# Moving two more GELU tiles to PSUM, and one more group of softmax heads to VectorE, in a fused attention and MLP kernel

## The chip, the cores and the metric

The kernel runs on one core of one Trainium2 chip. The core has TensorE (matmuls, PE in the profile), ScalarE (activation functions, ACT), VectorE (DVE), GpSimd (POOL) and SyncE (SP, which issues most DMAs). The metric is the device time of one execution in microseconds; the figure for the kernel before is the median of seven runs.

## The reference

The input x has 2048 rows of 448. After a layer norm (no learned scale), two branches are computed and combined:

```python
xn = _layernorm(x, axis=-1)
s = _A_ref(xn, A_wqkv, A_wo)                       # attention, 16 heads of 28
g = _silu(_B_ref(xn, B_w1, B_b1, B_w2, B_b2))      # MLP 448 -> 1792 -> 448
return x + s * g

# inside _A_ref
scores = jnp.einsum("bhqd,bhkd->bhqk", q, k) * scale
p = _softmax(scores, axis=-1)
o = jnp.einsum("bhqk,bhkd->bhqd", p, v)
# inside _B_ref
h = _gelu(jnp.einsum("bsd,df->bsf", x, w1) + b1)
return jnp.einsum("bsf,fd->bsd", h, w2) + b2
```

The scores are 16 x 2048 x 2048 numbers, each of which needs one exp.

## The kernel before, in words

**Tiling.** The scores are cut into 1024 pieces of 128 keys x 512 queries, called heads here and `m` in the code. A block is one group of four attention heads (`g`) and one chunk of 512 queries (`c`); there are 16 blocks of 64 heads, numbered in the order of work. Within a block four consecutive `m` are the same key tile for four attention heads, so that four numbers `4*q ... 4*q+3` form a group.

**Two ways to an exp.** Most heads go to ScalarE. `p_scores` lets TensorE write two or three heads side by side into one half of a PSUM ring of six banks (line 1217), and `p_exps` reads them with one exp and writes them as bf16 into a P slot (line 1273). The halves are banks 0 to 2 and 4 to 5, used in turn, so that the exps hold three and two heads in turn (only two while the first 64 heads are done). The groups named in `QUADS` go to VectorE in place of ScalarE. For each, `p_late` has single scores written to any free PSUM bank, or has them join a waiting task of `p_scores`; `p_apass` reads each bank once (line 1376), and `p_expq` makes an exp out of bit operations and a polynomial in five passes over 128 x 2048 numbers (lines 1427 to 1434). A group needs three work areas (`unit`), which are parts of buffers whose first use is over: x, w2 before it is loaded, the q and k weights, kT of blocks that are done. `step` leaves those groups out of the order of `p_scores`.

**PV and the end.** `p_pv` multiplies P by V into one PSUM bank (`acc`), eight heads at a time (line 1488). Groups from VectorE are added when they are ready, at the latest at the end of their block. Then the block is normalised, and after the last block of four the output projection is done (line 1585).

**The MLP.** The first layer makes 56 tiles of 128 x 512 (4 chunks x 14). The table of functions for gelu is another than the one for exp, so that all gelus run at once, in one stage in the middle, at about head 582 (`GM`). Before that stage, 36 of the tiles have been computed while exps ran, and VectorE has copied them from PSUM to `h` in SBUF (`p_f1`, line 1069). The other 20 are computed during the stage by `p_direct` (line 1086) into the ring, which no scores use then, and gelu reads them straight from PSUM. `PIECES` gives the order of gelu: an SBUF piece of five or four tiles, then a PSUM group (`None`) of three or two, and so on (`p_gelu`, line 1131). A PSUM group can be filled when the group two before it, which had the same half of the ring, has been read. Line 1136 loads the table for exp again. Then `p_f2` does the second layer beside the exps of the later blocks (line 1152), and `p_silu` makes the gate with a tanh (line 1167).

**Memory that is shared.** The part of `h` whose tiles come straight from PSUM isn't used before the gelu stage; until head 558 it gives 20 extra P slots beside the 18 of `P` (`pslots`, `p_room`). `room_free` holds the first PSUM gelu back until these have been used by PV. After gelu, xnT gives 15 more P slots.

**Order of work.** The program has no loops on the chip. A planner in Python (`run`, `start_of`, `put`) takes, of all tasks that could come next, the one with the earliest estimated start, and among those within 0.1 us the one with the lowest rank. Ranks that matter here: gelu -1, single scores for VectorE 0.9, scores for ScalarE 1, exp 3, direct tiles 3.5, first-layer tiles and second layer 5, PV 6 (1.2 when it lags far behind). When TensorE has been idle, filler matmuls on zeros (line 902) are put in by `p_busy`. In the gelu stage groups of VectorE may be begun up to 48 heads ahead (`GLEAD`). What the planner decides becomes a fixed order on each engine with semaphore waits between them, so a change of one list can alter the order of everything after it.

Of the kernel before, what the change touches and what calls it, by code (L numbers as in the profile page):

```python
# [19 lines left out]
C = 4  # L20
KT = 4
T = 16
FT = F // 128
WS = D + 4
NRING = 6
NP = 18
# [1 line left out]
MTOT = NBLK * T * 4  # L28

GM = 64 * 9 + 6  # L30
QUADS = (17, 22, 25, 35, 36, 50, 54, 65, 76, 84, 89, 99, 102, 116, 118, 132, 140, 142, 145, 152, 153, 162, 164, 179, 186, 194, 204, 210, 211, 214, 228, 233, 243)
SM_SCALE = DH ** -0.5
LOG2E = 1.4426950408889634
EXP_A3, EXP_A2, EXP_LC = 0.16391228, 0.00783292, 1.1187538523466403
# [2 lines left out]
KNORM = 2.5  # L37
PV_START = 5
HAM_WIN, HAM_LOW, DUM = 3.4, 0.85, 0.17
ND = 8  # L40
PIECES = [(0, 0, 5), None, (0, 5, 5), None, (0, 10, 4), None, (1, 0, 5), None, (1, 5, 5), None, (1, 10, 4), None,
          (2, 0, 4), None, (3, 10, 4), None]
SBT = [(c, ft) for c, f0, n in [p for p in PIECES if p] for ft in range(f0, f0 + n)]
SEM, OWN = 0.07, 0.03
SWITCH = 0.1
JOINT = 0.05
# [27 lines left out]
class _Kernel:  # L74
# [183 lines left out]
    def alloc(self):  # L258
# [3 lines left out]
        B = _Buf  # L262
# [99 lines left out]
        self.b_ox = [B() for _ in range(C)]  # L362
        hx = lambda c, f0, n: self.h[:, c, 512 * f0:512 * (f0 + n)].rearrange("p (k n) -> p k n", n=512)
        self.pslots = [(self.P[:, i0:i0 + n, :], k) for i0, n in ((0, NP),) for k in range(n)]
        self.pslots += [(hx(c, f, 10), k) for c, f in ((2, 4), (3, 0)) for k in range(10)]
        self.pslots += [(self.xnT[:, :, :].rearrange("p k (c n) -> p (k c) n", n=512), k) for k in range(16)]
        self.b_P += self.b_hf[2][4:14] + self.b_hf[3][0:10] + [B() for _ in range(16)]
        self.pon = [(0, NP)]
        self.b_nm = [[B(), B()] for _ in range(C)]
        self.b_selb = B()  # L370
# [13 lines left out]
    def schedule(self):  # L384
# [27 lines left out]
        K.pv_done = [False] * MTOT  # L412
        K.late = {4 * q + k for q in QUADS for k in range(4)}
        K.late_left = [sum(1 for q in QUADS if K.sub_of(4 * q) == b) for b in range(NBLK + 3)]
        K.late_on = False
# [24 lines left out]
        def nxt():  # L440
            nonlocal o
            o += 1.0
            return o
# [18 lines left out]
        K.spawn(K.p_qn(1), nxt())  # L462
        f1 = deque(SBT)
        for c in range(C):
# [625 lines left out]

    def directs(self):
        K = self
        out, left = [], [[2, 4], [3, 0]]
        for i in range(ND):
            b0 = 4 * ((K.gu - 1 + i) % 2)
            n = 2 if b0 else 3
            c, f0 = left[i // (ND // 2)]
            left[i // (ND // 2)][1] += n
            out.append((c, f0, n, b0))
        return out  # L1100

    def p_direct(self):
        K = self
        yield ("until", lambda: K.gu is not None and K.exp_u >= K.gu - 1)
        for i, (c, f0, nf, b0) in enumerate(K.directs()):
            yield ("until", lambda: K.exp_u >= K.gu - 1 + i if i < 2 else K.dir_read >= i - 1)
            for n in range(nf):
                for k in range(2):
                    yield K.t_f1(c, f0 + n, K.ring[:, b0 + n, :], K.b_ring[b0 + n], k, 3.5)
            K.dir_n += 1  # L1110

    def p_gelu(self):
        K = self
        yield ("until", lambda: K.gu is not None and K.exp_u >= K.gu and K.n_f1 == len(SBT))
        left = [FT] * C
        for q, pc in enumerate(PIECES):
            if pc:
                c, f0, n = pc
                src = K.h[:, c, 512 * f0:512 * (f0 + n)]
                rd = []  # L1120
            else:
                i = K.dir_read
                yield ("until", lambda: K.dir_n > i and K.room_free())
                c, f0, n, b0 = K.directs()[i]
                src = K.ring[:, b0:b0 + n, :].rearrange("p b n -> p (b n)")
                rd = K.b_ring[b0:b0 + n]
                for ft in range(f0, f0 + n):
                    K.hf_free(c, ft)
            dst = K.h[:, c, 512 * f0:512 * (f0 + n)]
            left[c] -= n  # L1130
            yield _Task(ACT, lambda eng, dst=dst, src=src: eng.activation(dst, src, ACTF.Gelu_apprx_tanh), rd,  # L1131
                        K.b_hf[c][f0:f0 + n] + ([K.b_h[c]] if left[c] == 0 else []),
                        0.4267 * n + (0.1 if pc else 0.06) + (1.3 if q == 0 else 0), 0.05, -1)
            if not pc:
                K.dir_read += 1
        K.prog[ACT].append(lambda eng: eng.preload_act_table_set("exp_and_others"))
        K.tE[ACT] += 1.3
        for b in K.b_fsb + K.b_sig:
            b.w = K.b_w1.w
            b.r = list(K.b_w1.r) + [K.b_w1pad.w] + K.b_w1pad.r  # L1140
        K.gelu_done = True

    def p_f2(self, c, t):
        K = self
        bank, tok = yield ("bank", lambda: K.b_h[c].tw is not None and K.ready([K.b_h[c], K.b_w2]) and K.dir_read == ND and (c < 2 or K.g_done[c - 2]))
        hv = K.h[:, c, :].rearrange("p (f n) -> p f n", n=512)
# [83 lines left out]
    def p_scores(self):  # L1230
        K = self
        u = 0
        while K.next_m < MTOT:
# [3 lines left out]
            if K.gu is not None and u == K.gu + 1:  # L1237
                yield ("until", lambda: K.dir_read == ND)
            b0 = 4 * (u % 2)
# [103 lines left out]
    def in_gelu(self):  # L1343
        return self.gu is not None and self.exp_u >= self.gu - 1 and self.dir_read < ND

    def p_late(self):
        K = self
        yield ("until", lambda: K.late_on)
        K.spawn(K.p_room(), 0)
        for q in QUADS:  # L1350
            m0 = 4 * q
# [30 lines left out]
    def p_room(self):  # L1382
        K = self
        yield ("until", lambda: K.stg_done == 2)
        for ft in range(10):
            K.hf_free(3, ft)
        K.pon += [(NP, 10), (NP + 10, 10)]
        yield ("until", lambda: K.next_m >= GM - 24)
        K.pon = K.pon[:1]
        yield ("until", lambda: K.gelu_done)  # L1390
        for b in K.b_P[NP + 20:]:
            for x in K.b_xnT:
                for y in x:
                    b.r += y.r
        K.pon.append((NP + 20, 15))

    def room_free(self):
        K = self
        return all(K.pv_done[m] for i, m in K.plast.items() if NP <= i < NP + 20)

    def assign(self, ms, b0):
        K = self
# [274 lines left out]
```

## Time and profile before

| | before |
|---|---|
| median of 7 runs | 462.34 us (462.14 to 462.75) |
| the profiled execution | 462.15 us |
| its span, first to last instruction | 460.3 us |
| busy: ScalarE, TensorE, VectorE | 448.5, 438.3, 368.1 us |
| exps (line 1273) | 363 instructions, 892 heads |
| gelus (line 1131) | 8 from SBUF, 8 from PSUM |
| gelu stage, table load to the first exp after | 245.2 to 273.1 us |
| granted TensorE clock | 0.998 of full speed |

Times in the profile are from the start of the span. A line of a group gives source line, engine, operation, tiles written and read, sizes and count; then the time in which any of the group was busy, the mean of one in ns, and the engine's idle time ahead of them with what ended it. Consecutive instructions of ScalarE overlap in the record: one ends after the next has begun. "h", "xnT" and "P" as the target of an exp are only the place of its P slot.

### The profile page before, as it was taken

How to read it: one execution, taken by the hardware profiler on the slowest of the kernel's cores; microseconds unless marked ns; L12 is line 12 of the kernel's file. 1: busy time of each engine (PE TensorE's matmuls, PEld its weight loads, DVE VectorE, ACT ScalarE, POOL GpSimd, SP SyncE). 2: the span in 40 equal slices, each digit the busy share in tenths (PEclk: the TensorE clock that was granted, in tenths of full speed). 3: DMA queues.
4: the chain of work that ended last, by engine and by line, in shares of the span. 5: the costliest groups of instructions: out<-in, count | busy, mean ns of one | idle time of the engine just before them, and what ended most of it. 6: DMA issues, size and time to landing. Idle time of an engine off the chain costs nothing.

```text
span 460.3 us, 10628 instructions
## 1 busy us (share of the span) xinstructions
PE 438.3 (95%) x4474; PEld 164.7 (36%) x4474; DVE 368.1 (80%) x577; ACT 448.5 (97%) x408; POOL 42.4 (9%) x85
## 2 busy tenths in 40 slices
PE   6999999999999999999999999999999999999995
PEld 5533333333323332323323333333333244343462
DVE  8956898898888898968888997157878689989675
ACT  6999999999999999999999999999999999999994
POOL 7470000001010000000000000000000100101011
PEclk9999999999999999999999999999999999999999
DMA  9701000000000000000040000000000010111131
GB/s 266 269 2 37 2 1 0 1 2 3 2 1 1 1 0 3 2 1 2 1 140 1 1 0 3 2 2 0 1 1 1 1 41 2 22 21 15 28 43 41
DMA packets 8048, 11.16 MB, mean 24 GB/s; under 512 B 1697, under 2 KB 6993, under 8 KB 7954
## 3 DMA queue, kind: packets, MB, share of 16 engines
q1 hardware_dynamic: 6850, 8.43, 6.0%
q0 software_dynamic: 864, 1.38, 2.3%
q8 instruction: 35, 0.57, 0.5%
q10 hardware_dynamic: 288, 0.69, 0.4%
q14 instruction: 11, 0.09, 0.1%
HBM read 8.61 MB, written 3.21 MB: 26 GB/s over the span
## 4 chain that ended last, share of the span: by engine, by line
PE 52%; ACT 34%; issue 10%; DVE 2%; DMA 1%; POOL 0%; ACTq 0%; DVEq 0%; POOLq 0%
ACT P L1273 16%; PE ring L1217 14%; ACT h L1273 11%; PE acc L1488 10%; PE ring L1086 6%; ACT xnT L1273 5%; PE ring L1152 4%; PE misc L1152 4%; PE acc L902 3%; PE misc L1086 2%; PE ring L741 1%; PE misc L741 1%; PE misc L1217 1%; PE misc L1585 1%; PE ring L1585 1%
## 5 line engine op out<-in xcount | busy, mean ns | idle before, releaser
L1273 ACT ACTIVATE P<-ring 128x1024 bf16<-128x1024 f32 (+1 forms) x194 | 224.0, 1264 | 1.1 <-PE ring L1217 0.8
L1217 PE MATMUL ring<-qT,kT 32*128 32x512 bf16 (+2 forms) x1072 | 142.5, 358 | 11.2 <-ACT P L1273 4.4
L1273 ACT ACTIVATE h<-ring 128x1024 bf16<-128x1024 f32 (+1 forms) x98 | 115.7, 1303 | 0.2
L1217 PEld LDWEIGHTS ring<-qT,kT 32*128 32x128 bf16 x1072 | 37.2, 91 | 133.3 <-ACT P L1273 57.9
L1273 ACT ACTIVATE xnT<-ring 128x1536 bf16<-128x1536 f32 (+1 forms) x71 | 84.8, 1286 | 0.1
L1488 PE MATMUL acc<-P,vaug 128*32 128x512 bf16 (+2 forms) x537 | 50.6, 357 | 0.4 <-ACT P L1273 0.4
L1086 PE MATMUL ring<-xnT,w 128*128 128x512 bf16 x152 | 40.2, 382 | 0.1
L1558 POOL CAST rhi<-rc 128x16 bf16<-128x16 f32 x15 | 6.9, 457 | 358.9 <-DVE rc L1556 194.5
L902 PE MATMUL acc<-ident,zero 128*128 128x128 bf16 x444 | 36.3, 220 | 0.0
L902 PEld LDWEIGHTS acc<-ident,zero 128*128 128x128 bf16 x444 | 25.3, 98 | 15.0 <-issue 13.6
L1217 PE MATMUL misc<-qT,kT 32*128 32x512 bf16 (+1 forms) x80 | 29.6, 374 | 0.0
L1376 DVE TENSOR_SCALAR x_sb<-misc 128x512 uint16<-128x512 f32 x34 | 23.3, 686 | 7.6 <-PE misc L1217 7.0
L1152 PE MATMUL misc<-w,h 128*128 128x448 bf16 x112 | 27.6, 356 | 0.2 <-DVE wk L1376 0.2
L1152 PE MATMUL ring<-w,h 128*128 128x448 bf16 x112 | 27.2, 355 | 0.3 <-DVE qT L980 0.3
L1488 PE MATMUL acc<-h,vaug 128*32 128x512 bf16 x243 | 25.9, 385 | 0.0
L1488 PE MATMUL acc<-xnT,vaug 128*32 128x512 bf16 (+2 forms) x236 | 21.2, 331 | 0.0
L1086 PE MATMUL misc<-xnT,w 128*128 128x512 bf16 x72 | 20.2, 383 | 0.0
L1546 DVE CAST E_sb<-acc 128x512 bf16<-128x512 f32 x15 | 10.4, 691 | 10.6 <-PE acc L1488 10.4
L1488 PEld LDWEIGHTS acc<-P,vaug 128*32 128x32 bf16 x537 | 13.0, 95 | 15.4 <-issue 11.1
L1086 PEld LDWEIGHTS ring<-xnT,w 128*128 128x128 bf16 x152 | 11.6, 97 | 17.5 <-issue 6.8
L1131 ACT ACTIVATE h<-h 128x2560 bf16<-128x2560 bf16 (+1 forms) x8 | 17.1, 2131 | 0.0
L1376 DVE TENSOR_SCALAR kT<-ring 128x512 uint16<-128x512 f32 x18 | 12.4, 686 | 5.6 <-PE ring L1217 5.6
(262 smaller groups left out, 655.0 us busy)
## 6 DMA issues: line engine op xcount, KB each, us to landing
w<-in_B_w_dram SPq DMA_DIRECT2D x1, 1568.0 KB, 7.3
w<-in_B_w_dram SPq DMA_DIRECT2D x1, 1344.0 KB, 8.8
out_dram<-in_A_x_dram SPq DMA_DIRECT2D x3, 448.0 KB, 11.9
out_dram<-h POOLq DMA_DIRECT2D x6, 224.0 KB, 3.9
x_sb<-in_A_x_dram SPq DMA_DIRECT2D x2, 448.0 KB, 5.1
h<-in_A_wqkv_dram SPq DMA_DIRECT2D x3, 168.0 KB, 4.9
x_sb<-in_A_x_dram ACTq DMA_DIRECT2D x1, 448.0 KB, 4.8
h<-in_A_x_dram SPq DMA_DIRECT2D x1, 448.0 KB, 3.4
```

Source lines behind the costliest of these rows:

```text
L741: ins = eng.matmul(bank, w[:, kt, g * 128:(g + 1) * 128], K.xnT[:, kt, c * 512:(c + 1) * 512], start=(kt == 0), stop=(kt == KT - 1))
L902: ins = eng.matmul(K.acc[:, 0:128], K.zero[:, :], K.ident[:, :], start=False, stop=True, skip_group_check=True)
L1086: ins = eng.matmul(bank, K.w1[:, kt, ft * 128:(ft + 1) * 128], K.xnT[:, kt, c * 512:(c + 1) * 512], start=(kt == 0), stop=(kt == KT - 1))
L1131: yield _Task(ACT, lambda eng, dst=dst, src=src: eng.activation(dst, src, ACTF.Gelu_apprx_tanh), rd, K.b_hf[c][f0:f0 + n] + ([K.b_h[c]] if ...
L1152: ins = eng.matmul(ps, hv[:, ft, t * 128:(t + 1) * 128], K.w2[:, ft, :], start=(ft == 0), stop=(ft == FT - 1))
L1217: return eng.matmul(dst, K.kT[32 * j:32 * j + 32, g, t * 128:(t + 1) * 128], K.qT[32 * j:32 * j + 32, g, c * 512 + q0:c * 512 + q0 + nq], ...
L1273: return eng.activation(reg[:, i0:i0 + n, :], K.ring[:, b0:b0 + n, :], ACTF.Exp, scale=SM_SCALE)
L1376: yield _Task(DVE, lambda eng: eng.tensor_scalar(K.unit[u][:, 512 * k:512 * k + 512].bitcast(dt.uint16), bank, SM_SCALE * LOG2E * 128.0, ( ...
L1488: return eng.matmul(K.acc[32 * j:32 * j + 32, q0:q0 + nq], K.vaug[:, t, 4 * g + j, :], ap[:, col:col + nq], tile_position=(0, 32 * j), sta ...
L1546: yield _Task(DVE, lambda eng: eng.tensor_copy(E, K.acc[:, :]), [K.b_acc], [tE], 0.7, 0.0, 0)
L1558: yield _Task(POOL, lambda eng: eng.tensor_copy(K.rhi[:, :], K.rc[:, :]), [K.b_rc], [K.b_rhl], 1.1, 0.0, 1)
L1585: ins = eng.matmul(ps, K.qT[:, g, c * 512 + t * 128:c * 512 + (t + 1) * 128], K.wo[:, g, :], start=(g == 0), stop=(g == G - 1))
```

## The change

- PSUM groups of gelu: nine in place of eight (`ND`), with 22 tiles in place of 20. Groups alternate between three and two tiles, and the last takes what is left.
- SBUF pieces: 34 tiles in place of 36, in pieces of 5, 5, 5, 4, 4, 4, 4, 3. Pieces now run over the flat index of the 56 tiles and may cross a chunk's border; the tiles from PSUM are the last 22. The last two gelus are both PSUM groups.
- The extra P slots before gelu are 22 (8 + 14) in place of 20 (10 + 10).
- `QUADS`: 34 groups in place of 33. Twelve are kept (17, 22, 25, 36, 65, 99, 142, 152, 153, 164, 194, 211), 22 have new places. Blocks 3, 8 and 9 have one, four and four groups in place of two, three and three; the other blocks have as many as before.

```diff
-QUADS = (17, 22, 25, 35, 36, 50, 54, 65, 76, 84, 89, 99, 102, 116, 118, 132, 140, 142, 145, 152, 153, 162, 164, 179, 186, 194, 204, 210, 211, 214, 228, 233, 243)
+QUADS = (17, 22, 25, 36, 37, 59, 65, 72, 82, 87, 99, 103, 115, 122, 129, 135, 138, 142, 152, 153, 157, 158, 164, 168, 178, 180, 194, 199, 211, 213, 222, 229, 234, 242)
...
-ND = 8
-PIECES = [(0, 0, 5), None, (0, 5, 5), None, (0, 10, 4), None, (1, 0, 5), None, (1, 5, 5), None, (1, 10, 4), None,
-          (2, 0, 4), None, (3, 10, 4), None]
-SBT = [(c, ft) for c, f0, n in [p for p in PIECES if p] for ft in range(f0, f0 + n)]
+ND = 9
+PIECES, F0 = [], 0
+for n in (5, 5, 5, 4, 4, 4, 4, 3):
+    PIECES += [(F0, n), None]
+    F0 += n
+PIECES += [None] * (ND - PIECES.count(None))
+SBT = [(f // FT, f % FT) for f in range(F0)]
...
-        self.pslots += [(hx(c, f, 10), k) for c, f in ((2, 4), (3, 0)) for k in range(10)]
+        self.pslots += [(hx(2, F0 - 28, 42 - F0), k) for k in range(42 - F0)] + [(hx(3, 0, 14), k) for k in range(14)]
...
     def directs(self):
         K = self
-        out, left = [], [[2, 4], [3, 0]]
+        out, f = [], F0
         for i in range(ND):
             b0 = 4 * ((K.gu - 1 + i) % 2)
-            n = 2 if b0 else 3
-            c, f0 = left[i // (ND // 2)]
-            left[i // (ND // 2)][1] += n
-            out.append((c, f0, n, b0))
+            n = min(2 if b0 else 3, 56 - f)
+            out.append((f, n, b0))
+            f += n
+        assert f == 56
         return out
...
-        K.pon += [(NP, 10), (NP + 10, 10)]
+        K.pon += [(NP, 42 - F0), (NP + 42 - F0, 14)]
...
-        return all(K.pv_done[m] for i, m in K.plast.items() if NP <= i < NP + 20)
+        return all(K.pv_done[m] for i, m in K.plast.items() if NP <= i < NP + 56 - F0)
```

`p_direct` and `p_gelu` are changed to the flat index in the same way.

More of the change, by code (lines that the diff above doesn't have):

```diff
@@ L364, in alloc @@
         self.pslots = [(self.P[:, i0:i0 + n, :], k) for i0, n in ((0, NP),) for k in range(n)]
-        self.pslots += [(hx(c, f, 10), k) for c, f in ((2, 4), (3, 0)) for k in range(10)]
+        self.pslots += [(hx(2, F0 - 28, 42 - F0), k) for k in range(42 - F0)] + [(hx(3, 0, 14), k) for k in range(14)]
         self.pslots += [(self.xnT[:, :, :].rearrange("p k (c n) -> p (k c) n", n=512), k) for k in range(16)]
-        self.b_P += self.b_hf[2][4:14] + self.b_hf[3][0:10] + [B() for _ in range(16)]
+        self.b_P += self.b_hf[2][F0 - 28:14] + self.b_hf[3] + [B() for _ in range(16)]
         self.pon = [(0, NP)]
@@ L1104, in p_direct @@
         yield ("until", lambda: K.gu is not None and K.exp_u >= K.gu - 1)
-        for i, (c, f0, nf, b0) in enumerate(K.directs()):
+        for i, (f0, nf, b0) in enumerate(K.directs()):
             yield ("until", lambda: K.exp_u >= K.gu - 1 + i if i < 2 else K.dir_read >= i - 1)
@@ L1108, in p_direct @@
                 for k in range(2):
-                    yield K.t_f1(c, f0 + n, K.ring[:, b0 + n, :], K.b_ring[b0 + n], k, 3.5)
+                    yield K.t_f1((f0 + n) // FT, (f0 + n) % FT, K.ring[:, b0 + n, :], K.b_ring[b0 + n], k, 3.5)
             K.dir_n += 1
@@ L1115, in p_gelu @@
         left = [FT] * C
+        hf = K.h[:, :, :].rearrange("p c f -> p (c f)")
         for q, pc in enumerate(PIECES):
             if pc:
-                c, f0, n = pc
-                src = K.h[:, c, 512 * f0:512 * (f0 + n)]
+                f0, n = pc
+                src = hf[:, 512 * f0:512 * (f0 + n)]
                 rd = []
@@ L1123, in p_gelu @@
                 yield ("until", lambda: K.dir_n > i and K.room_free())
-                c, f0, n, b0 = K.directs()[i]
+                f0, n, b0 = K.directs()[i]
                 src = K.ring[:, b0:b0 + n, :].rearrange("p b n -> p (b n)")
                 rd = K.b_ring[b0:b0 + n]
[L1127 to L1130, printed above, removed]
+                for f in range(f0, f0 + n):
+                    K.hf_free(f // FT, f % FT)
+            dst = hf[:, 512 * f0:512 * (f0 + n)]
+            for f in range(f0, f0 + n):
+                left[f // FT] -= 1
+            wr = [K.b_hf[f // FT][f % FT] for f in range(f0, f0 + n)]
+            wr += [K.b_h[c] for c in range(C) if left[c] == 0 and K.b_h[c].tw is None]
             yield _Task(ACT, lambda eng, dst=dst, src=src: eng.activation(dst, src, ACTF.Gelu_apprx_tanh), rd,
-                        K.b_hf[c][f0:f0 + n] + ([K.b_h[c]] if left[c] == 0 else []),
-                        0.4267 * n + (0.1 if pc else 0.06) + (1.3 if q == 0 else 0), 0.05, -1)
+                        wr, 0.4267 * n + (0.1 if pc else 0.06) + (1.3 if q == 0 else 0), 0.05, -1)
             if not pc:
@@ L1384, in p_room @@
         yield ("until", lambda: K.stg_done == 2)
-        for ft in range(10):
+        for ft in range(14):
             K.hf_free(3, ft)
-        K.pon += [(NP, 10), (NP + 10, 10)]
+        K.pon += [(NP, 42 - F0), (NP + 42 - F0, 14)]
         yield ("until", lambda: K.next_m >= GM - 24)
@@ L1390, in p_room @@
         yield ("until", lambda: K.gelu_done)
-        for b in K.b_P[NP + 20:]:
+        for b in K.b_P[NP + 56 - F0:]:
             for x in K.b_xnT:
@@ L1394, in p_room @@
                     b.r += y.r
-        K.pon.append((NP + 20, 15))
+        K.pon.append((NP + 56 - F0, 15))
     def room_free(self):
         K = self
-        return all(K.pv_done[m] for i, m in K.plast.items() if NP <= i < NP + 20)
+        return all(K.pv_done[m] for i, m in K.plast.items() if NP <= i < NP + 56 - F0)
     def assign(self, ms, b0):
```

## The prediction

> **What bounds the kernel now.** I read the page's busy shares first, then ScalarE's instructions in order of time, then the busy time by stretch, and last the groups of VectorE and TensorE.
>
> ```profile
> span 460.3 us, 10628 instructions
> PE 438.3 (95%) x4474; PEld 164.7 (36%) x4474; DVE 368.1 (80%) x577; ACT 448.5 (97%) x408; POOL 42.4 (9%) x85
> ```
>
> ScalarE (ACT) is busy in all but 11.8 us of the span, and those lie almost wholly before its first exp at 12.6 us and after its last at 453.6 us. TensorE's 95% is less telling: 36.3 us of it are the filler matmuls of line 902. VectorE has 460.3 - 368.1 = 92.2 us free. So the time is ScalarE's work plus ScalarE's stalls. The busy column hides the stalls, because one exp's recorded end overlaps the next one's start; the true price of an instruction is the distance between two starts.
>
> ```profile
> 118.08 1.60 ACT L1273 ACTIVATE h<-ring 128x1536 bf16<-128x1536 f32 x1
> 119.41 1.18 ACT L1273 ACTIVATE P<-ring 128x1024 bf16<-128x1024 f32 x1
> 120.31 1.62 ACT L1273 ACTIVATE h<-ring 128x1536 bf16<-128x1536 f32 x1
> ...
> 261.68 1.47 ACT L1131 ACTIVATE h<-ring 128x1536 bf16<-128x1536 f32 x1
> 263.01 1.94 ACT L1131 ACTIVATE h<-h 128x2048 bf16<-128x2048 bf16 x1
> 264.81 1.05 ACT L1131 ACTIVATE h<-ring 128x1024 bf16<-128x1024 f32 x1
> 265.71 1.94 ACT L1131 ACTIVATE h<-h 128x2048 bf16<-128x2048 bf16 x1
> 267.63 1.45 ACT L1131 ACTIVATE h<-ring 128x1536 bf16<-128x1536 f32 x1
> 268.97 1.90 ACT L1131 ACTIVATE h<-h 128x2048 bf16<-128x2048 bf16 x1
> 270.77 1.01 ACT L1131 ACTIVATE h<-ring 128x1024 bf16<-128x1024 f32 x1
> 271.81 1.28 ACT L1136 ACT_TABLE_LOAD   x1
> ```
>
> The columns are start, duration, engine, line and tile. An exp of three heads takes 1.33 us from start to start (118.08 to 119.41), one of two heads 0.90. That is 0.427 per head and 0.05 per instruction, so one of a single head is 0.48. The gelu on PSUM costs the same (1.33, 0.90). On SBUF four tiles take 1.80 and five 2.23, which is 0.427 per tile and 0.093 per instruction, so three tiles are 1.37. The piece at 265.71 took 1.92 instead of 1.80: the PSUM group behind it was 0.12 us late. The last group before the table load lost another 0.13 us.
>
> Over the whole run the intervals of the 363 exps add up to 406.7 us. At the clean prices they would be 166 x 1.33 + 197 x 0.903 = 398.7. So **8.1 us are stalls**, some 40 of them of 0.06 to 0.42 us, nearly all behind a two-head exp, when the three scores that follow were not there within 0.9 us. By stretches of 20 us they run from 0.07 to 0.62 us with a scatter of 0.16.
>
> **The ScalarE work.** Walking the loop of heads with the new list gives 34 x 4 = 136 heads on VectorE instead of 132, and 888 on ScalarE instead of 892. They go in 165 exps of three, 196 of two and one of a single head: 165 x 1.33 + 196 x 0.903 + 0.48 = 396.9, so **-1.76 us**. The gelus before are four of 2.23, four of 1.80, four of 1.33 and four of 0.90, together 25.04. After, the unit at which gelu starts falls on the other half of the ring, so the nine groups hold 2, 3, 2, 3, 2, 3, 2, 3, 2 tiles (22). With SBUF pieces of 5, 5, 5, 4, 4, 4, 4, 3: 6.68 + 7.20 + 1.37 + 4 x 1.33 + 5 x 0.903 = 25.09, **+0.05 us**. The table loads stay two. ScalarE's own work shrinks by 1.71 us, and as it is the bound over the whole stretch from 12.6 to 453.6 us, all of it lies on the path.
>
> **The VectorE work.** One more group of four heads costs four reads of PSUM and five passes over SBUF; two tiles fewer are copied out of PSUM.
>
> ```profile
> L1376 DVE TENSOR_SCALAR x_sb<-misc 128x512 uint16<-128x512 f32 x34 | 23.3, 686 | 7.6 <-PE misc L1217 7.0 <-PE ring L1217 0.4
> L1069 DVE CAST h<-ring 128x512 bf16<-128x512 f32 x18 | 12.4, 688 | 2.6 <-PE ring L1086 2.3
> L1427 DVE TENSOR_SCALAR x_sb<-w 128x2048 uint16<-128x2048 uint16 x5 | 3.4, 687 | 0.0
> L1431 DVE TENSOR_TENSOR x_sb<-x_sb,kT 128x2048 f16<-128x2048 bf16 x4 | 4.9, 1219 | 0.0
> ```
>
> The third column after the count is the mean in ns. 4 x 0.686 + 3 x 0.687 (lines 1427, 1429, 1432) + 2 x 1.219 (1431, 1434) = 7.24 us more, 2 x 0.688 = 1.38 less: +5.9 us, which lies in VectorE's 92.2 us of idle time and costs nothing as long as it is not all in one place. The new list puts four groups in block 8 and four in block 9, where the old one had three and three. Block 8's four take 29.0 us while ScalarE needs 44 heads x 0.447 = 19.7 us to the block's end, so they end about 9 us late, inside the 27.9 us from 245.2 to 273.1 in which no exp runs. Block 9's four then end near 245 + 9 + 29 + 3 (other work) = 286 us. ScalarE would stall on that only once the 33 P slots are used up. Only the block's last eight heads hold theirs for a late group, which leaves 29 slots, 13 us, counted from block 10's first exp near 290. So that cover is some 17 us deep.
>
> **The TensorE work.** The direct tiles need the same four matmuls as before, only later: two tiles, 1.73 us, move from the time before gelu into the gelu stage. That is the one stage where TensorE has nothing to spare.
>
> ```profile
> 244.30:271.80 27.50, 27.49 (x160) 9.32 (x160) 24.66 (x35) 27.46 (x18) 0.75 (x2) 1.00 0.00 1
> ```
> ```profile
> 248.09 1.03 PE L1086 MATMUL ring<-xnT,w 128*128 128x512 bf16 x4
> 249.05 0.39 PE L1217 MATMUL misc<-qT,kT 32*128 32x512 bf16 x1
> 249.37 1.04 PE L1086 MATMUL ring<-xnT,w 128*128 128x512 bf16 x4
> ```
>
> The first line gives busy time by engine in the gelu stretch: TensorE (the second number) 27.49 of 27.50, weight loads 9.32. [...] But adding up the starts in this stretch fills it: 80 direct matmuls at 0.216 are 17.3; 13 single scores are 5.5 (four matmuls and one score take 249.37 - 248.09 = 1.28 us, so the score takes 0.42); 56 PV matmuls in 14 rounds of 0.216 with their switches are about 4.0; the rest is 0.7. Together 27.5. [...]
>
> After, until the last direct group is due: 22 x 0.864 = 19.0, scores of up to four groups 6.7, PV 4.0, rest 0.7: 30.4 us. The time there is: ScalarE's exp of three heads before gelu instead of two adds 0.43 and the gelus add 0.05 to the 26.5 us (244.3 to 270.8) of before, so 26.9. What must come first by the planner's ranks, scores and direct tiles, is 25.7 and fits with 1.2 to spare; PV ranks behind and can slip into the time after 273 us. So the late groups cost between nothing and 30.4 - 26.9 = 3.5 us. I take **+0.2**, nearest to the 0.25 of before, since the ninth group has no SBUF piece ahead of it: ScalarE reaches it 1.37 + 1.33 = 2.7 us after its ring half came free, and it needs 1.73 us of matmuls beside a possible rest of the eighth.
>
> **The moved groups.** 22 of the 34 groups have new places, and with them every later instruction is ordered anew. Where a score or a PV step now falls decides the small stalls. No row shows these places. I take the present rate, 8.1 / 33 = **+0.25** for one more group. From both sides: two samples of 22 stretches with a scatter of 0.16 differ by 0.16 x sqrt(44) = 1.1 us, two thirds of the groups moved, so about 0.9 either way.
>
> No transfer is added or dropped. The one that the groups can delay is w2's load (it waits for three work areas): the page's row of GB/s shows it between 230 and 242 us, and line 1152 first uses it at 272.9, so 30 us hide it.
>
> **Sum.** -1.76 + 0.05 + 0.2 + 0.25 = -1.26. The profiled execution took 462.15 us (span 460.3 and 1.85 around it), so 460.9; the median of the seven runs lies 0.19 higher, which gives 461.1.
>
> **Rivals.** About 0.2%, 0.9 us, is what a measurement here tells from no change.
> 1. *The forecast:* ScalarE's 1.7 us are gained and stalls take less than half: 459.4 to 461.4. For it: 97% and a bound that holds from end to end. Chance 0.60.
> 2. *Stalls take the rest:* the new places cost 0.8 to 2.6 us more than the old ones, 461.4 to 463.3, typically 462.2. For it: 40 stalls in places that a planner's estimate had not foreseen. Against: it needs one scatter more than I take. Chance 0.20.
> 3. *Slower, TensorE becomes the bound in the gelu stage:* PV does not slip, each direct group is late, and the whole 3.5 us appear: -1.7 + 0.25 + 3.5 = +2.05, 464.4. It decides once TensorE's other work in the 26.9 us exceeds 26.9 - 19.0 + 2.4 = 10.3 us (2.4 is the stall that brings the time over 463.3); the list above makes it 11.4 at most. Against: the ranks. Chance 0.14.
> 4. *Slower, VectorE late:* block 9's groups end over 17 us later than I reckon and exps wait for slots; 2 us past that point is 463 to 465. Chance 0.06.
>
> **The numbers.** Faster 0.60, same 0.20, slower 0.20. The likeliest time is 461.1, its own range 459.4 to 461.4 (leaning to the upper end, as the unknown stalls do). Over all cases 459.4 to 463.8 leaves out about a tenth at each end.
>
> **What would show it.** Right: 362 exps and 17 gelus at the same prices, nine PSUM gelus of two and three in turn, first exp still at 12.6 us, stalls of 7.5 to 9.5 us. Step by step: late groups show as SBUF gelus longer than 1.80 or 2.23 from start to start; PV that slipped as fewer PV matmuls in the gelu stretch. Wrong: stalls outside 7 to 10 us; a gelu stage over 28.5 us from table load to the first exp (27.9 now); or a tail after the last exp that is not 6.7 us.

## The result and the profile after

The changed kernel takes **461.02 us** (median of 13 runs, 460.76 to 461.40) against 462.28 us for the kernel before (33 runs taken over the study). The ratio of the means is 0.9969, 95% interval 0.9962 to 0.9977. Ratios here and below are of the means of runs in the faster of the two states that were seen, which leaves out one run, the slowest of e12. The forecast was 461.1. First the page of the changed kernel, whose profiled execution took 461.40 us, the upper end of its runs:

```profile
span 459.5 us, 10615 instructions
PE 436.5 (95%) x4431; PEld 162.5 (35%) x4431; DVE 373.4 (81%) x584; ACT 446.8 (97%) x408; POOL 40.9 (9%) x85
```

ScalarE is 1.7 us less busy and VectorE 5.3 us more. The end of the gelu stage, ScalarE in order of time (start, duration, line, tiles):

```profile
268.24 1.94 ACT L1138 ACTIVATE h<-h 128x2048 bf16<-128x2048 bf16 x1
270.04 1.05 ACT L1138 ACTIVATE h<-ring 128x1024 bf16<-128x1024 f32 x1
270.94 1.52 ACT L1138 ACTIVATE h<-h 128x1536 bf16<-128x1536 bf16 x1
272.31 2.40 ACT L1138 ACTIVATE h<-ring 128x1536 bf16<-128x1536 f32 x2
274.74 1.28 ACT L1142 ACT_TABLE_LOAD   x1
```

The prices hold: 1.80 for four SBUF tiles, 0.90 for two PSUM tiles, 1.37 for the new piece of three. The last two groups, 272.31 to 274.74, take 2.43 us where 1.33 + 0.90 are due, so the ninth group lost 0.19 us. Every other gelu ran on time. Next the gelu stretch: busy time by engine, then TensorE's direct tiles with the idle time ahead of them.

```profile
247.30:274.70 27.40, 26.46 (x144) 9.48 (x143) 24.81 (x35) 27.37 (x19) 0.00 (x0) 1.00 0.00 1
```
```profile
L1089 PE MATMUL ring<-xnT,w 128*128 128x512 bf16 x87 | 21.0, 381 | 0.9 <-ACT h L1138 0.9
```

TensorE was idle for 0.94 us here, waiting for ScalarE to free the ring. Before, it was idle for 0.01 us in a stretch as long.

The account of ScalarE, made of the distances between starts in both traces:

| us | before | after | change | forecast |
|---|---|---|---|---|
| first exp begins | 12.56 | 13.17 | +0.61 | 0 |
| exps at clean prices | 398.67 | 396.92 | -1.75 | -1.76 |
| stalls of exps | 8.07 | 8.52 | +0.45 | +0.25 |
| gelus at clean prices | 25.04 | 25.09 | +0.05 | +0.05 |
| late gelus | 0.28 | 0.21 | -0.07 | +0.2 |
| last exp's end to the end | 6.69 | 6.63 | -0.06 | 0 |

With the tanhs, which take 0.02 us less, this gives the -0.80 us between the two spans. The start varies from profile to profile whatever the kernel: over the fourteen profiles of this study the first exp begins between 12.56 and 13.17 us, and these two happen to be the ends. Without it the account says -1.41; the medians say -1.26.

### The profile page after: what moved, and what is told of

Its sections match the earlier page's. It is cut to its first block, busy times and chain, and to the rows that moved or that the text cites. A ratio compares the mean times of both kernels' runs of the same rounds, so it can differ in the third digit from the quotient of the medians.

```text
span 459.5 us, 10615 instructions
## 1 busy us (share of the span) xinstructions
PE 436.5 (95%) x4431; PEld 162.5 (35%) x4431; DVE 373.4 (81%) x584; ACT 446.8 (97%) x408; POOL 40.9 (9%) x85
## 4 chain that ended last, share of the span: by engine, by line
PE 47%; ACT 38%; issue 11%; DVE 3%; POOL 1%; ACTq 0%; DVEq 0%; POOLq 0%
ACT P L1279 18%; PE ring L1223 13%; ACT xnT L1279 9%; ACT h L1279 9%; PE acc L1494 8%; PE ring L1089 5%; PE ring L1158 3%; PE misc L1158 3%; PE acc L905 3%; PE misc L1089 2%; PE misc L744 2%; PE ring L744 2%; PE acc L887 1%; PE misc L1223 1%; PE ring L1031 1%
## 5 line engine op out<-in xcount | busy, mean ns | idle before, releaser
L1279 ACT ACTIVATE P<-ring 128x1024 bf16<-128x1024 f32 (+1 forms) x188 | 217.6, 1265 | 1.4 <-PE ring L1223 1.0
L1223 PE MATMUL ring<-qT,kT 32*128 32x512 bf16 (+2 forms) x1074 | 145.1, 358 | 11.4 <-ACT P L1279 5.6
L1279 ACT ACTIVATE h<-ring 128x1024 bf16<-128x1024 f32 (+1 forms) x102 | 117.8, 1268 | 0.2
L1494 PE MATMUL acc<-P,vaug 128*32 128x512 bf16 (+2 forms) x524 | 49.2, 358 | 0.0
L905 PE MATMUL acc<-ident,zero 128*128 128x128 bf16 x393 | 34.3, 221 | 0.0
L905 PEld LDWEIGHTS acc<-ident,zero 128*128 128x128 bf16 x393 | 22.3, 98 | 18.8 <-issue 18.2
L1494 PE MATMUL acc<-h,vaug 128*32 128x512 bf16 x248 | 27.6, 384 | 0.0
L1382 DVE TENSOR_SCALAR x_sb<-misc 128x512 uint16<-128x512 f32 x31 | 21.3, 687 | 6.2 <-PE misc L1223 5.9
L1089 PE MATMUL misc<-xnT,w 128*128 128x512 bf16 x68 | 19.5, 383 | 0.5 <-DVE qT L1581 0.5
L1494 PE MATMUL acc<-xnT,vaug 128*32 128x512 bf16 (+2 forms) x240 | 18.7, 330 | 0.9 <-ACT P L1279 0.7
L1138 ACT ACTIVATE h<-h 128x2048 bf16<-128x2048 bf16 (+2 forms) x8 | 16.2, 2030 | 0.0
```

Of the source, the lines that this page charges most:

```text
L905: ins = eng.matmul(K.acc[:, 0:128], K.zero[:, :], K.ident[:, :], start=False, stop=True, skip_group_check=True)
L1089: ins = eng.matmul(bank, K.w1[:, kt, ft * 128:(ft + 1) * 128], K.xnT[:, kt, c * 512:(c + 1) * 512], start=(kt == 0), stop=(kt == KT - 1))
L1223: return eng.matmul(dst, K.kT[32 * j:32 * j + 32, g, t * 128:(t + 1) * 128], K.qT[32 * j:32 * j + 32, g, c * 512 + q0:c * 512 + q0 + nq], ...
L1279: return eng.activation(reg[:, i0:i0 + n, :], K.ring[:, b0:b0 + n, :], ACTF.Exp, scale=SM_SCALE)
L1382: yield _Task(DVE, lambda eng: eng.tensor_scalar(K.unit[u][:, 512 * k:512 * k + 512].bitcast(dt.uint16), bank, SM_SCALE * LOG2E * 128.0, ( ...
L1494: return eng.matmul(K.acc[32 * j:32 * j + 32, q0:q0 + nq], K.vaug[:, t, 4 * g + j, :], ap[:, col:col + nq], tile_position=(0, 32 * j), sta ...
```

## Experiments

Several theories went in. **W**: the time follows ScalarE's work, and a group costs a fixed 0.25 us of stalls wherever it is. **The rivals**: the gelu part brings the gain (G), the new places do (P), or TensorE's time in the gelu stage decides (T). All kernels in one table; "work" is the exps at clean prices, "stage" runs from the table load to the first exp after it. Work, stalls and stage sum to the span less 25.6 to 26.5 us in every kernel, so what differs is in these columns. They are of the profiled execution. In e9, e10 and e12, whose executions differ much, that was a long one (464.62, 463.09 and 466.87 us).

| kernel | median | ratio to before | work | stalls | stage | span |
|---|---|---|---|---|---|---|
| before | 462.28 | | 398.67 | 8.07 | 27.91 | 460.3 |
| the change | 461.02 | 0.9969 | 396.92 | 8.52 | 27.88 | 459.5 |
| e1_gelu_only | 468.53 | 1.0128 (1.0113 to 1.0144) | 398.67 | 11.29 | 30.97 | 466.9 |
| e2_groups_only | 472.23 | 1.0209 (1.0195 to 1.0223) | 396.92 | 19.66 | 27.83 | 470.2 |
| e3_one_less | 464.10 | 1.0032 (1.0020 to 1.0045) | 398.67 | 9.92 | 27.89 | 462.3 |
| e4_old_plus_one | 470.99 | 1.0183 (1.0169 to 1.0197) | 396.92 | 18.23 | 27.91 | 469.5 |
| e5_even | 487.22 | 1.0542 (1.0526 to 1.0557) | 396.92 | 34.81 | 27.88 | 485.7 |
| e6_even_ahead | 468.43 | 1.0135 (1.0120 to 1.0150) | 396.92 | 16.04 | 27.88 | 466.7 |
| e7_short_passes | 472.11 | 1.0213 (1.0198 to 1.0228) | 396.92 | 19.68 | 27.82 | 470.0 |
| e8_direct28 | 474.92 | 1.0275 (1.0258 to 1.0292) | 396.92 | 13.81 | 36.36 | 472.9 |
| e9_short_fillers | 461.20 | 0.9998 (0.9971 to 1.0025) | 396.92 | 12.26 | 27.88 | 462.8 |
| e10_fewer_fillers | 461.09 | 0.9975 (0.9962 to 0.9988) | 396.92 | 10.48 | 27.88 | 461.3 |
| e11_short_layer2 | 484.76 | 1.0485 (1.0466 to 1.0504) | 396.92 | 33.26 | 27.82 | 484.2 |
| e12_35_fitted | 465.50 | 1.0035 (1.0000 to 1.0070) | 395.11 | 15.49 | 28.08 | 465.1 |

### Each part alone

e1_gelu_only: the changed kernel with the old list. e2_groups_only: the kernel before with the new list.

```diff
 # e1, against the changed kernel
-QUADS = (17, 22, 25, 36, 37, 59, 65, ...
+QUADS = (17, 22, 25, 35, 36, 50, 54, ...
 # e2, against the kernel before: the same line the other way round
```

> The nine PSUM groups and the new pieces alone, with the old 33 groups of VectorE. The whole computation is done. Theory W (the time follows ScalarE's own work): that work is 423.77 us against 423.72 before, so the time stays within 0.5 us of 462.3. Theory G (the gelu part brings the gain, since two copies fewer leave VectorE free and the eight-plus-fourteen P slots are more): 0.5 to 1.3 us faster. Theory T (TensorE has nothing to spare in the gelu stage): up to 3.5 us slower, seen as gelus that start late.

> The 34 new groups alone, with the old pieces and eight PSUM groups. The whole computation is done. Theory W: ScalarE's work falls by 1.76 us, stalls rise by 0 to 0.9, so 460.6 to 461.5, the same as the whole change within 0.5 us. Theory G (the groups need the relief that the gelu part gives VectorE): the gain is half or less, 461.7 or more, with exps that wait for late scores or slots between 200 and 320 us.

Both are far slower than either kernel: 6.2 and 10.0 us over before. W falls with this, and G too: no part brings the gain, and each alone brings a loss. ScalarE's work is as reckoned in both; the loss is stalls. In e1 3.0 us of it are in the gelu stage, as T had it. ScalarE in order of time, with its idle time and what ended it in brackets:

```profile
268.31 1.45 ACT L1138 ACTIVATE h<-ring 128x1536 bf16<-128x1536 f32 x1 [0.71 <-PE ring L1089]
269.66 1.48 ACT L1138 ACTIVATE h<-h 128x1536 bf16<-128x1536 bf16 x1
271.40 1.02 ACT L1138 ACTIVATE h<-ring 128x1024 bf16<-128x1024 f32 x1 [0.27 <-PE ring L1089]
273.98 1.02 ACT L1138 ACTIVATE h<-ring 128x1024 bf16<-128x1024 f32 x1 [1.55 <-PE ring L1089]
```

The last three groups wait for their direct tiles, and the ninth, which has no SBUF piece ahead of it, waits longest. So the stage can be short of TensorE's time by 3 us with the same number of direct tiles as in the change. Between the two table loads the changed kernel has less else for TensorE to do: 40 PV matmuls beside tiles and scores, where e1 has 56 and eleven others (projections, sums and fillers).

The rest of the loss in e1, and most of it in e2, is few and long waits. The longest in e2, all engines in order of time:

```profile
306.28 1.13 ACT L1273 ACTIVATE xnT<-ring 128x1024 bf16<-128x1024 f32 x1
...
308.76 2.81 PE L1152 MATMUL ring<-w,h 128*128 128x448 bf16 x14
...
310.22 1.22 DVE L1434 TENSOR_TENSOR wk<-wk,x_sb 128x2048 bf16<-128x2048 f16 x1
...
311.67 0.39 PE L1488 MATMUL acc<-P,vaug 128*32 128x512 bf16 x1
...
312.85 1.45 ACT L1273 ACTIVATE xnT<-ring 128x1536 bf16<-128x1536 f32 x1 [5.44 <-PE acc L1488]
```

The exp at 312.85 waits 5.44 us for PV to give back the P slot that it will write (its target is a slot in xnT). PV of the block's end needs the block's last group, whose fifth pass (line 1434) ends at 311.44. Meanwhile TensorE does second-layer matmuls. This is the form of e2's three long stalls and of the longest in e1 (2.1 us at 364 us): the exps have run out of P slots, and the PV that would free them stands at the end of its block. A stall of 0.8 us at 332 us in e1 is a wait for scores.

### One group less, one group more

```diff
 # e3, against the changed kernel
-... 211, 213, 222, 229, 234, 242)
+... 211, 213, 229, 234, 242)
 # e4, against the kernel before
-... 153, 162, 164, 179, 186, ...
+... 153, 162, 164, 171, 179, 186, ...
```

> The changed kernel without group 222, which goes back to ScalarE; 33 groups. The whole computation is done. Theory W: ScalarE's work is 1.76 us more, stalls 0.25 less, so 1.5 us over the changed kernel: 462.5. Theory P (it is the new places that stall less, and the number of groups matters little): within 0.5 us of the changed kernel, 461.0 to 461.5.

> The kernel before with one group more, number 171, put by hand in the middle of the widest gap of its list; nothing else is changed. The whole computation is done. Theory W: 1.76 us less work and about 0.25 more stalls: 460.8 (460.0 to 461.6). Theory P (the gain needs all the new places): the stalls take half or more of it, 461.5 to 463.

e3 is 3.1 us over the changed kernel. 1.75 of that is work, as W had it, but the stalls rise by 1.4 although there is a group less. P, which had it within 0.5 us of the changed kernel, falls too. In e4 a single group, put by hand into the widest gap, costs 8.7 us net. One wait holds most of it:

```profile
337.79 2.81 PE L1152 MATMUL ring<-w,h 128*128 128x448 bf16 x14
340.53 0.61 PE L1488 MATMUL acc<-P,vaug 128*32 128x512 bf16 x7
340.64 0.62 DVE L1157 TENSOR_TENSOR w<-ring,b2b 128x448 bf16<-128x448 f32 x1 [0.62 <-PE ring L1152]
341.30 1.70 ACT L1167 ACTIVATE w<-w 128x1792 bf16<-128x1792 bf16 x1 [8.39 <-DVE w L1157]
```

The tanh of the second layer stands first in ScalarE's fixed order there and waits for VectorE's bias additions (line 1157), two of which stand behind two groups' passes. The last of them, at 340.64, has to wait for TensorE's fourteen second-layer matmuls. The tanh is only the first in line, though. PV of block 10's end begins at 340.53, right behind the same fourteen matmuls and 0.5 us after the added group's last pass (338.8 to 340.0), and ScalarE's exps come after the tanh.

### Even places, late and early

```diff
 # e5 and e6, against the changed kernel
-QUADS = (17, 22, 25, 36, ..., 234, 242)
+QUADS = (17, 24, 31, 37, ..., 235, 242)
 # e6 in addition
-LEAD, WAIT, GLEAD = 0, 3.0, 48
+LEAD, WAIT, GLEAD = 24, 3.0, 48
```

> The changed kernel with its 34 groups at even distances (17, 24, 31, ... 242). The whole computation is done, and ScalarE's own work is 422.0 us, as in the changed kernel. Theory L (a list is good only if no block's PV has to wait for its last VectorE group while ScalarE runs out of P slots; the list on trial was fitted for that): exps wait for PV several times, by more than 1 us each, stalls of 15 to 35 us, 468 to 488 us. Theory R (stalls go by the number of groups, and the four single misfits so far are accidents): stalls of 8 to 12 us, 461 to 465.

> The same even list, but each group may be begun 24 heads (some 11 us) before the scores reach it, instead of 0. The whole computation is done, ScalarE's own work is the same 422.0 us. Theory L: a group's work of 7.2 us is then done before its block ends, the waits of exps for PV go, stalls fall to 10 to 20 us, 463 to 472, at least 8 us faster than the even list begun late. Theory R, or VectorE simply short of time: no more than 3 us between the two.

Even places stall for 34.8 us, four times as much as the change's list with the same 34 groups. The longest waits of ScalarE, summed by what ended them (us in total, times, longest), first e5, then e6:

```profile
ACT P L1279 <- PE acc L1494: 19.5, 6, 12.2
ACT w L1173 <- DVE w L1163: 3.6, 1, 3.6
```
```profile
ACT P L1279 <- PE ring L1223: 5.6, 5, 4.3
```

e5's exps wait for PV, 19.5 us in six waits. With the groups begun 24 heads earlier no exp waits for PV any more, and the stalls fall by 18.8 us. The planner ordered everything anew for e6, so it is not one wait that was taken away; but the kind of wait that theory L names is the kind that went. e6's longest wait, 4.3 us, is for scores that TensorE begins at 36.86, right after VectorE has written a piece of qT (36.05 to 36.80); whether an early group put them there stays open.

### Who holds PV: VectorE or TensorE's order

e7_short_passes keeps e2's order on every engine and makes three of a group's five passes short.

```diff
-eng.tensor_tensor(W.bitcast(f16), W, D1.bitcast(f16), ALU.mult)
+eng.tensor_tensor(W[:, 0:256].bitcast(f16), W[:, 0:256], D1[:, 0:256].bitcast(f16), ALU.mult)
 # lines 1429 and 1434 in the same way; lines 1427 and 1432 in full
```

> The new groups with the old gelu part (472.2 us), with the instructions of every engine in the same order, but three of VectorE's five passes of a group on 256 of 2048 columns, so that a group costs VectorE some 2.6 us less; the weights of the groups are wrong by that. If VectorE's time is what PV waits for in the long stalls (5.7, 2.0 and 2.6 us at 306, 337 and 419 us of that kernel), each shrinks by about 2 us or goes: 465 to 468. If TensorE's fixed order is (PV stands behind matmuls of the second layer that were put ahead of it), they stay: 471 to 472.5.

Nothing moves: 472.11 against 472.23 us, and each long stall is within 0.02 us of e2's. The same place in e7:

```profile
308.74 2.81 PE L1152 MATMUL ring<-w,h 128*128 128x448 bf16 x14
308.94 0.62 DVE L1157 TENSOR_TENSOR w<-misc,b2b 128x448 bf16<-128x448 f32 x1 [1.76 <-PE misc L1152]
310.20 0.29 DVE L1434 TENSOR_TENSOR wk<-wk,x_sb 128x256 bf16<-128x256 f16 x1
311.38 0.33 PE L902 MATMUL acc<-ident,zero 128*128 128x128 bf16 x3
311.65 0.39 PE L1488 MATMUL acc<-P,vaug 128*32 128x512 bf16 x1
312.83 1.45 ACT L1273 ACTIVATE xnT<-ring 128x1536 bf16<-128x1536 f32 x1 [5.45 <-PE acc L1488]
```

The last pass now ends at 310.49, 0.95 us earlier, and PV begins when it did before. VectorE can't even use all the time it saves, as a bias addition ahead of its fourth pass waits 1.76 us for TensorE. TensorE has second-layer matmuls and three fillers to do that stand ahead of PV in its order. A faster VectorE can't change that. So in these waits VectorE's speed is ruled out, and the rows put the fixed order in its place; no run moved PV forward to show it directly. In e5's 12.2 us wait the two can't be told apart: the last group's fifth pass ended at 173.37 and PV began at 173.50, with the five passes spread over 9.6 us between copies of q, k and the first layer, and with first-layer matmuls on TensorE right ahead of PV.

e11_short_layer2 was to confirm it by shortening what stands ahead of PV.

```diff
 # e11, in addition to e7
-ins = eng.matmul(ps, hv[:, ft, ...], K.w2[:, ft, :],
+ins = eng.matmul(ps[:, 0:64], hv[:, ft, ...], K.w2[:, ft, 0:64],
```

> As e7_short_passes (the instructions of every engine in the order of e2_groups_only, three of five VectorE passes short), and in addition the matmuls of the second layer on 64 of 448 columns, so that fourteen of them take about 1 us in place of 2.8; that layer is left out but for these columns. If the long stalls are PV that stands behind second-layer matmuls in TensorE's fixed order, the stalls of 5.7 and 2.0 us at 306 and 337 us shrink by half or more, and the time is 463 to 469. If they stay above 5 and 1.7 us, something else holds PV, and the time is 471 or more.

It settles nothing: between 270 and 380 us TensorE was busy for 93.63 us in place of 108.34 and was granted a clock of 0.64 in place of 1.00, and the whole middle slowed down. The stretch of the second layer in e11 and then in e2 (the first number is TensorE's busy time, the third from the end its granted clock):

```profile
270.00:380.00 110.00, 93.63 (x865) 33.39 (x863) 52.84 (x98) 91.48 (x78) 1.97 (x6) 0.64 0.00 1
```
```profile
270.00:380.00 110.00, 108.34 (x1014) 39.51 (x1013) 80.63 (x110) 102.13 (x88) 3.77 (x8) 1.00 0.02 4
```

Matmuls that were not shortened take longer there: two scores into the ring took 0.61 us at 307.93 in e11 and 0.39 at 307.67 in e2. Stalls rise from 19.7 to 33.3 us.

### TensorE's time in the gelu stage

```diff
 # e8, against the changed kernel
-ND = 9
+ND = 12
-for n in (5, 5, 5, 4, 4, 4, 4, 3):
+for n in (4, 3, 3, 2, 2, 2, 2, 2, 2, 2, 2, 2):
```

> The changed kernel with 28 of the 56 tiles straight from PSUM in twelve groups, and twelve SBUF pieces of 4, 3, 3 and nine times 2 tiles. The whole computation is done. What tells the theories apart is the gelu stage, from the table load to the first exp after it; without late groups it would be 28.2 us. If TensorE's time is what limits it: 28 x 0.864 = 24.2 for the tiles and 14 single scores at 0.42 = 5.9, together 30.1 against 27.8 that ScalarE leaves, so groups are 2.3 us late in sum, up to 6 with PV between them: a stage of 30.5 to 34 us. If TensorE has the headroom that its weight loads show: no late groups, a stage of 28.2 to 28.7. The time of the whole kernel also holds what the groups stall after the stage and is no measure of this.

The stage takes 36.4 us, 8.2 us over the 28.2 of clean prices and 2.4 over the upper end of what was expected. Busy time in that stretch, and one late group:

```profile
246.40:281.90 35.50, 35.50 (x251) 13.31 (x248) 33.09 (x46) 28.09 (x26) 1.28 (x2) 1.00 0.00 1
```
```profile
271.29 1.45 ACT L1138 ACTIVATE h<-ring 128x1536 bf16<-128x1536 f32 x1 [2.86 <-PE ring L1559]
```

TensorE is busy for 35.50 of 35.50 us while weight loads show 13.31 (37%), and ScalarE idles 7.4 us for it. Here weight-load time does not show the headroom; the count of matmul starts does. The expected count was too low all the same, as it had left PV, the end of a block and even fillers out of the stage: none of these stayed behind the direct tiles as their ranks would have them.

### Fillers

Are the many small stalls scores that stand behind fillers?

```diff
 # e9: one filler in place of three; e10: the same, only up to head 768
-            for _ in range(3):
+            for _ in range(1):
```

> The changed kernel with one filler matmul in place of three each time that TensorE would be idle; the order of all else is the same. The fillers add zeros, so the result is the same. If the 8.5 us of small stalls behind two-head exps are scores that stand behind fillers: 1 to 4 us faster, 457 to 460. If they stand behind real work (PV, projections, second layer): within 0.5 us of 461.0, unless TensorE's granted clock falls below 0.99, which would make it slower.

> The changed kernel with one filler matmul in place of three up to head 768, and three after it; the order of all else is the same, and the fillers add zeros. In e9_short_fillers the exps up to about 382 us stalled 0.66 us less than in the changed kernel (6.87 against 7.53 us for the first 300), and only after that did the granted clock fall. If the fillers' delay of scores is real, and the clock stays at 1.0 since real work keeps TensorE busy until then: 460.2 to 460.7, with stalls of 7.8 to 8.0 us. If the 0.66 us is scatter between profiles: 460.9 to 461.2.

Partly. In e9 the first 300 exps stall 0.66 us less, with no difference in order. That is not scatter between profiles: e3, which has the changed kernel's list up to group 222, stalls as long there as the changed kernel does, 7.53 us in both. But the granted clock fell. Eight of e9's twelve runs take 460.9 to 461.6 us, at a mean clock of 0.986 to 0.994, the other four 464.6 to 465.6, at 0.975 to 0.979. One of the four, and then the changed kernel, between 380 and 400 us:

```profile
380.00:400.00 20.00, 17.86 (x157) 5.30 (x149) 14.65 (x22) 16.48 (x15) 3.12 (x4) 0.74 0.21 38
```
```profile
380.00:400.00 20.00, 18.77 (x237) 7.47 (x229) 17.31 (x27) 20.00 (x18) 3.12 (x4) 1.00 0.27 47
```

The clock falls to 0.74 on average, and ScalarE idles 3.5 us for scores. e10 was to keep the gain and avoid this, and fails: the clock falls elsewhere, and not as far in every execution (0.990 to 0.998 over its twelve runs). These lie between 460.07 and 463.17 us; the lowest is 0.7 under the lowest of the changed kernel, the median is the same. In the profiled one (463.09) it is 0.60 from 50 to 51 us and 0.50 from 51 to 53, and again 0.50 from 246 to 248. e10 between 46 and 50 and between 50 and 56 us, then the changed kernel:

```profile
46.00:50.00 4.00, 2.77 (x31) 1.10 (x29) 2.98 (x7) 4.00 (x5) 0.41 (x2) 1.00 0.00 0
...
50.00:56.00 6.00, 6.00 (x68) 1.90 (x66) 4.31 (x7) 4.29 (x5) 0.00 (x0) 0.72 0.00 0
```
```profile
46.00:50.00 4.00, 3.56 (x45) 1.54 (x37) 3.17 (x6) 4.00 (x4) 0.35 (x2) 1.00 0.00 0
50.00:56.00 6.00, 5.99 (x80) 2.28 (x80) 5.50 (x8) 5.86 (x6) 0.06 (x1) 1.00 0.01 3
```

Four microseconds with TensorE 2.77 us busy instead of 3.56 are followed by a slower clock, and one exp comes 1.9 us late.

### More groups, fitted anew

```diff
 # e12, against e10
-QUADS = (17, 22, 25, 36, 37, 59, ..., 229, 234, 242)      # 34
+QUADS = (18, 20, 28, 39, 43, 56, ..., 226, 240, 245)      # 35
-LEAD, WAIT, GLEAD = 0, 3.0, 48
+LEAD, WAIT, GLEAD = 16, 3.0, 48
```

> 35 groups, with places fitted anew to the planner's order (all but a few places differ from both lists), begun up to 16 heads ahead, with the nine PSUM groups, and with the fillers of e10_fewer_fillers. The whole computation is done. ScalarE's own work is 420.2 us, 1.8 less than in the changed kernel. Theory L (any number of groups does, provided that the list is fitted to the order): stalls of 7.5 to 9.5 us, 458.3 to 460.3. Theory G (34 is what VectorE can take: 373 + 7 us of work, and more late groups): exps wait for PV, stalls over 10.5 us, 461 or more.

In 5 of the 12 runs it takes 460.5 to 461.8 us, at a mean clock of 0.991 to 0.995, in the others 464 to 468, at 0.971 to 0.984: the profiled one has 12.6 us of stalls before gelu, with the clock at 0.50 from 44 to 60 us and at 0.75 from 60 to 68. After gelu, at a clock of 1.00, its 151 exps stall 2.88 us, and no exp waits long for PV. So a fitted list of 35 doesn't run out of slots where e4's 34 did, which speaks for L. With the fillers cut in the same kernel the time is no answer. The list with full fillers was not run, and whether it beats the change stays open.

## Why the prediction was right, and where it was not

**The number.** 461.02 against 461.1. The sum was -1.26 and the medians differ by 1.26. So close a hit is luck: the late gelus came 0.27 us under the forecast and the stalls 0.20 over it, and the two profiled executions differ by 0.80. That distances between starts are ScalarE's prices held: 1.33 us for three heads in the change (237.60 to 238.93) as in e4, e5 and e11, and 0.90 for two in the change (236.70 to 237.60) as in e1 and e2. That ScalarE is the bound from the first exp to the last held in the kernel before and in the changed one; in the slow ones other engines set long stalls.

**ScalarE's work.** -1.76 and +0.05 were forecast; -1.75 and +0.05 came.

**VectorE's work.** 5.9 us more were forecast, 5.3 came, hidden as said. The cover of blocks 8 and 9 held: no exp of the changed kernel waited for PV there.

**TensorE in the gelu stage.** +0.2 was forecast, -0.07 came. PV did slip (56 matmuls to 40), and five times two single scores ran side by side, which my price of 0.42 for each did not have. The bounds of 0 and 3.5 us were right for 22 tiles (0.21 in the change, 3.3 in e1), and e8 bore out the choice to go by matmul starts.

**The moved groups: the step that failed.** The forecast took the present 8.1 / 33 = 0.25 us per group, "about 0.9 either way". +0.45 came, inside that range, but by luck: the reasoning was wrong. The stalls aren't a rate per group, and the scatter of the 20 us stretches of a list that works says nothing of a list that doesn't. One group more cost 10.2 us of stalls (e4), one less 1.4 (e3), the same list under another gelu part 11.1 (e2), even places 26.3 (e5). The spread over these four, 1.4 to 26.3 us and all of it upward, is up to some thirty times the 0.9 that I gave. That this list stalls no more than the old one can't be seen in the profile before. The likeliest reading of the runs is that each list was fitted to the order that comes out with it, since every departure in places that was not fitted stalled more; how the two lists were made is not shown.

**The rivals.** Rival 2 (stalls take the rest) did not come up: the stalls rose by 0.45 us, under its 0.8. Rival 3 (TensorE in the gelu stage) is real, in e1 and e8, and did not come up in the change. Rival 4 (late groups use up the P slots) had the smallest chance, 0.06. It is the form of nearly all the long stalls in e1, e2, e4 and e5, at other places than the one that I had reckoned, and where the rows could tell (e2, e4, e7) behind TensorE's order and not for want of VectorE's time. A mechanism that was excluded at one place by a margin of 17 us was not looked for at the others.

## What to carry to other kernels

Where a planner fixes the order of all engines from a list of choices, the work on the engine that bounds could be forecast to 0.1 us here, but the stalls belong to the list and the code together. A part of such a change, or a neighbour of its list, may be slower than both ends, so test it whole and give the forecast a wide slow side. Look for long stalls where a buffer is given back in order: there the question is what stands ahead of the release on its engine, and a faster producer may not help, as e7 shows. Before taking out filler matmuls whose cost in sight is small (0.66 us here), look at the granted clock with and without them: between 380 and 400 us it was 1.00 in the changed kernel and 0.74 in e9, with one filler in place of three.

## What the runs showed of the hardware that was not expected

In the profiled execution of e10 TensorE's granted clock was 1.00 from 46 to 50 us and 0.50 from 51 to 53, without a long gap ahead of it: TensorE's longest between 46 and 50 us is 0.57 us, and it was busy for 69% of these 4 us. In the kernel before and in the changed one TensorE is busy for 81% or more of every 4 us that begin on a full us from 12 to 446, and the clock is 1.00 in all of them. In e12 the clock was 0.50 from 44 to 60 us, in e9 0.74 on average from 380 to 400.

The clock differs between executions of one program: its mean over e10's runs lies between 0.990 and 0.998, over e12's between 0.971 and 0.995. How little work, or how long a gap, is followed by a slower clock is not shown by these runs.

The price is large: e12 took 460.49 us at a mean clock of 0.992 and 466.97 at 0.976, and e11, at 0.903 to 0.909, took 12.7 us longer than e7, which has more to do, at 0.995 to 0.998.
